# In the first chunk, ScalarE copies instead of DMAs fill two tiles' fixed value blocks, and the first two weight blocks are asked for earlier on GpSimd's queue

## The chip, the cores and the metric

The kernel runs on one core of one Trainium2 chip. The metric is the device time of one execution in microseconds (us); less is better. The core's engines run side by side, each in its own program order: TensorE (PE: matmuls, and PEld: the weight load ahead of each), VectorE (DVE), ScalarE (ACT), GpSimd (POOL) and SyncE (SP, which here only issues DMAs). They wait for each other on semaphores. Sixteen DMA engines move data between memory (HBM) and SBUF. POOL's DMAs go through the queue that the profile calls q0, SP's through q1; q8 carries instructions (75 packets of together 1.23 MB in this run).

## The reference

Block-sparse attention over 4 batches, 8 heads, 768 positions in 24 blocks of 32, then a two-layer network on its output:

```python
mask = |blk_i - blk_j| <= 1  or  blk_i in (0, 23)  or  blk_j in (0, 23)  or  blk_j in sampled_blocks[blk_i]
scores = where(mask, q @ k.T / sqrt(64), -1e9)
attn = softmax(scores)            # each row's sum + 1e-9 divides it
x = attn @ v                      # to [3072, 512]
out = relu(x @ w_in) ** 2 @ w_out # w_in 512 x 2048, w_out 2048 x 512
```

A query block so attends to the two fixed blocks 0 and 23, to three sampled blocks and to a window of three neighbours; the blocks 0 and 23 as queries attend to all keys. The weights come as float64 and are turned into float32 on the chip.

## The kernel before

A batch has 6 tiles of 128 queries; 3 tiles make a chunk, and there are 8 chunks. Everything is issued in an order written out by hand. The program first does the attention of chunk 0 alone (the tiles 0, 1 and 2 of batch 0, and the four head pairs of the "whole" queries), then for each chunk the network, with the next chunk's attention strewn between its matmuls. In the first part a half tile (`Half`, four heads) passes through scores (`s`, PE, L405), maxima (`m`, DVE, L417), exponentials (`p`, ACT, L464), transposes (`pt`, PE, L479), copies (`pT`, ACT, L489), the product with the values (`pv`, PE, L515) and the division (DVE). A whole query pair (`Whole`) passes through `g`, `mg`, `pg`, `ptg`, `pTg` and `pvg` in the same way; its `pTg` is copied half by ACT and half by DVE (L675). The loop over `work` at the end issues these stages in steps of `now`.

The values of tile k stand in two SBUF tiles, `V[k][0]` and `V[k][1]`. For each of 4 query blocks j there are, in rows of 32: in the first the two fixed blocks (rows 0 to 63) and two sampled ones, in the second a sampled one and the window. In the order listings V_83 and V_84 are the two of tile 0, V_127 and V_128 of tile 1, V_129 and V_130 of tile 2. Who fills them in chunk 0:

- SP's DMAs (q1), in this order: the query tiles q_0 and q_1, the fixed blocks of tile 0 for j = 0 (`load_static`, L214), its window (L313), the sampled blocks of tiles 0 and 1 (`load_sampled`, L327: 9 and 12 DMAs of 32 rows each), the fixed blocks of tiles 1 and 2 (`load_static`, two DMAs of 64 rows by 4 blocks j by 520 columns, which read the same 64 rows of `v` four times), q_2, and the sampled blocks of tile 2 (12 DMAs). Each of SP's DMAs reuses one of eight semaphores in turn and so waits until the DMA eight before it has landed.
- ACT: for tile 0 it copies the fixed blocks from j = 0 to j = 1, 2, 3 (`copy_static`, L221, two copies, one for each half of the heads). The list `fixed` is worked off at one entry per step from step 7 on. Later ACT places 12 window blocks of tile 1 (L229).
- POOL: the other window blocks (L229).

POOL also issues the loads of keys and values (`KN`, `vn`), copies sampled keys from `KN` to `KG` (`copy_keys`, L301 and L281), and asks for the weight blocks. `cut_next` (L786 for the DMA) handles one step of a row of weight blocks of 512 KB each: it loads one (`craw`, on POOL's queue) and turns the one loaded five steps earlier (ACT L802 and L804, then DVE L813 and L814, then the splits). The first five calls stand between POOL's copies of keys and windows and only load; the later ones stand in the `work` loop from step 35 on. At the change the program reads:

```python
    load_sampled(1, 0, nc.sync, SP)
    for k in range(1, UC):
        load_static(k, k // 2)
    load_q(0, 2, own=begin)
...
    for k in range(2):
        deque(copy_keys(0, k), 0)
    for i in range(AHEAD + 1):
        if i == FIRST_LOADS:
            for f, *at in windows[1, 0]:
                f(*at, nc.gpsimd.tensor_copy)
```

The network of chunk 0 begins with the transposes `xt` (L872), their copies `xh`, `xl` (L875, L876) and the first matmuls `ph` (L886); `po` (L915, L926) is its second layer.

Of the kernel before, what the change touches and what calls it, by code (L numbers as in the profile page):

```python
# [48 lines left out]
UC = 3  # L49
# [4 lines left out]
AHEAD = 5  # L54
# [29 lines left out]
LATE = (0, 4)  # L84
KEYS_N = 2
MOVED = 6


WO_LOW = 3
# [8 lines left out]
def tile_block_sparse_attention_moe(ctx: ExitStack, tc, kd, knd, qd, qgd, vd, vnd, samp, const, wcat, out):  # L98
# [86 lines left out]
    def values_of(k):  # L185

        return V[k if k < UC else 0]
# [4 lines left out]
    def halves(k, u):  # L192

        if k < UC:
            return slice(0, 2) if u == k // 2 else None
        return slice(u, u + 1)

    def columns(src, us):

        n = HW // 2  # L200
        return src[..., us.start * n : us.stop * n]

    def places(v, rows, js, us):

        return columns(v[rows, js].rearrange("p j u c -> p j (u c)"), us)

    def load_static(k, u, eng=nc.sync):
        us = halves(k, u)
        if us is None:
            return  # L210
        n = 1 if k == 0 else NJ
        src = columns(vd[order[k][0], V_STATIC * BLK :], us)
        src = src.unsqueeze(1).broadcast_to([2 * BLK, n, src.shape[-1]])
        eng.dma_start(places(values_of(k)[0], slice(0, 2 * BLK), slice(0, n), us), src)  # L214
# [40 lines left out]
    def load_q(b, t, eng=nc.sync, own=None):  # L255
        q = (own or rot).tile([P, NJ, NPAIR, BLK], F32, tag="q", name=f"q{b}_{t}", bufs=1 if own else 2)
        n = NJ * NPAIR * BLK
        eng.dma_start(q.rearrange("p a b c -> p (a b c)"), qd[b, :, t * n : (t + 1) * n])
        st["q", b, t] = q
# [9 lines left out]
    def copy_keys(b, t, own=None):  # L269

        vals = sampled(t, 0, POOL)
        kg = keys_of(b, t, own)
        for us in (slice(0, 1), slice(1, 2)) if t == 0 else (slice(0, 2),):
            if t < UC:
                for u in range(us.start, us.stop):
                    static_keys(b, t, u, nc.gpsimd.tensor_copy)
            for j in sorted(groups(t)):
                for r in range(NRAND):
                    to = kg[:, j, 2 + r].rearrange("p (u i) s -> p u (i s)", u=2)
                    of = KN.rearrange("p u k i s -> p u k (i s)")  # L280
                    nc.gpsimd.tensor_copy(to[:, us].unsqueeze(2), of[:, us, bass.ds(vals[NRAND * j + r], 1)])  # L281
                yield
# [32 lines left out]
    def load_sampled(k, u, eng, on):  # L315
        us = halves(k, u)
        if us is None:
            return
        b, t = order[k]
        VA, VB = values_of(k)  # L320
        vals = sampled(t, 1, on)
        v4 = columns(vd[b], us).rearrange("(a p) c -> p a c", p=BLK)
        for j in sorted(groups(t)):
            for r in range(NRAND):
                at = slice(0, BLK) if r == 2 else slice((2 + r) * BLK, (3 + r) * BLK)
                dst = places(VB if r == 2 else VA, at, slice(j, j + 1), us)
                eng.dma_start(dst, v4[:, bass.ds(vals[NRAND * j + r], 1)])  # L327
# [10 lines left out]
    def written(b, t):  # L338

        parts[b, t] = parts.get((b, t), 0) + 1  # L340
        whole = 2 + (NPAIR if t in (0, NT - 1) else 0)
        if parts[b, t] < whole or order.index((b, t)) < MOVED:
            return
# [9 lines left out]
    class Half:  # L353


        def __init__(self, b, t, u):
            self.b, self.t, self.u = b, t, u
            self.k = order.index((b, t))
            self.moved = self.k >= MOVED
            self.name = f"{b}_{t}_{u}"  # L360
# [469 lines left out]
    def cut_next():  # L830

        nonlocal done
        n = len(cuts)
        for stage, lag in ((cut, AHEAD), (cut_bits, AHEAD + 1), (cut_split, AHEAD + 2), (cut_load, 0)):
            if 0 <= done - lag < n:
                stage(*cuts[done - lag])
        done += 1
# [21 lines left out]
    def turn(c):  # L859
# [3 lines left out]
        for i in range(UC):  # L863
            if c * UC >= MOVED:
                while full:
# [129 lines left out]
    load_q(0, 1)  # L995
    load_sampled(0, 0, nc.sync, SP)
    load_sampled(1, 0, nc.sync, SP)
    for k in range(1, UC):
        load_static(k, k // 2)
    load_q(0, 2, own=begin)  # L1000
    load_sampled(2, 1, nc.sync, SP)
    windows = {
# [1 line left out]
        for k in range(1, UC)  # L1004
        for u in range(2)
    }
    for k in range(2):
        deque(copy_keys(0, k), 0)
    for i in range(AHEAD + 1):
# [3 lines that stand above are left out]
        if i == SECOND_LOADS:  # L1013
            deque(copy_keys(0, 2, begin), 0)
        if i == THIRD_LOADS:
            for f, *at in windows[2, 0] + windows[2, 1]:
                f(*at, nc.gpsimd.tensor_copy)
        if i < AHEAD:
            cut_next()
    fixed = [(copy_static, 0, i) for i in range(2)]  # L1020
    moves = windows[1, 1]
    side = lambda name: ps_o.tile([P, 512], F32, tag="o", name=name)
    work = Stream()
# [97 lines left out]
```

## Time and profile before

| | |
|---|---|
| timed runs | 746.91 us median of 3 (742.52, 746.91, 747.28) |
| the profiled execution | 743.47 us in all, of which the span of its instructions is 741.7 us |
| busy in the span | PE 713.3 us (96%), ACT 510.3, DVE 509.1, POOL 485.4 |
| attention of chunk 0 alone | from 0 to 58.25 us, when the first `ph` matmul starts |
| HBM traffic | 85.59 MB read, 6.29 MB written |
| granted TensorE clock | 0.995 of full speed over the span |

How to read the rows: a timeline row has the start and the length of a stretch of like instructions, in us from the start of the span, then engine, line, operation, what is written and read, the shape and the count; in brackets the idle time of the engine ahead of it, and what ended that. "issue" there means that the engine waited for nothing that the profile shows. A row of windows has a stretch, its length, each engine's busy time and, in brackets, how many of its instructions started in it, then the granted clock, the busy share of the DMA engines and the rate. A row of a DMA queue has packets, MB and the share of the 16 DMA engines' time in the stretch that was asked for. Most fp32 matmuls of the program are two in the records, transposes one.

### The profile page before, as it was taken

To read this page: it belongs to the slowest core of one execution; us is meant where nothing else is said; L and a number is where in the kernel's file an instruction comes from. 1 tells how busy PE (TensorE), PEld (TensorE's weight loads), DVE (VectorE), ACT (ScalarE), POOL (GpSimd) and SP (SyncE) were. 2 spreads that over 40 slices of the span, in tenths; PEclk is the share of its full clock that TensorE was granted. 3 is DMA by queue.
4 is the path that set the end of the run, shared out by engine and by line. 5 is a ranking of instruction groups with operands and counts; after the bars stand their busy time and mean duration, and the time that the engine had idled before them with its cause. 6 is when DMAs were issued, how large, how long until landed. Compare 5 with 4: busy or idle time off the path is not lost.

```text
span 741.7 us, 25152 instructions
## 1 busy us (share of the span) xinstructions
PE 713.3 (96%) x9440; PEld 591.5 (80%) x9440; DVE 509.1 (69%) x980; ACT 510.3 (69%) x1130; POOL 485.4 (65%) x592
## 2 busy tenths in 40 slices
PE   5779999999999999999999999999999999999997
PEld 2557676668888888887888888877888888889896
DVE  5776886767866866778876676778877677545342
ACT  3777887998867775689866777479876777623222
POOL 5984534237876565758767566677866566767784
PEclk9999999999999999999999999999999999999999
DMA  8986889643533535533444345534344342101001
GB/s 279 235 224 186 262 256 331 150 116 107 141 82 96 144 90 168 155 86 113 105 125 106 98 118 166 158 86 141 93 126 105 89 131 53 33 2 43 1 1 43
DMA packets 84861, 93.54 MB, mean 126 GB/s; under 512 B 13539, under 2 KB 70628, under 8 KB 84740
## 3 DMA queue, kind: packets, MB, share of 16 engines
q1 hardware_dynamic: 78788, 69.09, 35.3%
q0 software_dynamic: 5664, 22.45, 9.3%
q8 instruction: 75, 1.23, 0.7%
q14 instruction: 46, 0.38, 0.2%
q10 hardware_dynamic: 288, 0.39, 0.1%
HBM read 85.59 MB, written 6.29 MB: 124 GB/s over the span
## 4 chain that ended last, share of the span: by engine, by line
PE 84%; DVE 4%; ACT 4%; issue 1%; ACTq 0%; DVEq 0%
PE ph L886 35%; PE po L926 31%; PE s L405 6%; PE pv L500 5%; PE po L915 4%; PE pvg L689 1%; PE g L621 1%; DVE xl L876 1%; ACT craw L804 1%; DVE WO L814 1%; DVE m L417 0%; PE pv L515 0%; DVE WO L813 0%; PE pt L479 0%; ACT p L464 0%
## 5 line engine op out<-in xcount | busy, mean ns | idle before, releaser
L450 ACT ACTIVATE pm<-p 32x256 f32<-32x256 f32 x528 | 219.2, 415 | 17.3 <-DVE p L425 9.6
L849 POOL TENSOR_TENSOR wo<-WO,wo 128x512 fp32r<-128x512 f32 x112 | 144.8, 1293 | 61.3 <-DVE wo L848 60.0
L849 POOL TENSOR_TENSOR wi<-W,wi 128x512 fp32r<-128x512 f32 x104 | 135.1, 1299 | 66.8 <-ACT wi L846 32.8
L886 PE MATMUL ph<-xh,wi 128*128 128x384 f32 x832 | 175.6, 348 | 2.0 <-DVE wi L848 1.7
L926 PE MATMUL po<-wo,gh 128*128 128x512 f32 x672 | 176.2, 397 | 0.0
L890 ACT ACTIVATE r<-ph 128x384 f32<-128x384 f32 x128 | 62.7, 490 | 162.8 <-PE ph L886 162.1
L905 POOL TENSOR_TENSOR gl<-gf,gh 128x384 fp32r<-128x384 f32 x112 | 113.8, 1016 | 85.1 <-DVE gf L902 73.1
L886 PEld LDWEIGHTS ph<-xh,wi 128*128 128x128 f32 x832 | 146.9, 188 | 22.8 <-issue 10.1
L902 DVE SCALAR_TENSOR_TENSOR gf<-ph,r 128x384 f32<-128x384 f32 x112 | 62.3, 556 | 147.3 <-ACT r L890 142.6
L926 PEld LDWEIGHTS po<-wo,gh 128*128 128x128 f32 x672 | 123.8, 188 | 24.4 <-issue 4.0
L926 PE MATMUL po<-wo,gl 128*128 128x512 f32 x336 | 98.3, 401 | 0.0
L886 PE MATMUL ph<-xl,wi 128*128 128x384 f32 x416 | 90.4, 339 | 0.0
L926 PEld LDWEIGHTS po<-wo,gl 128*128 128x128 f32 x336 | 62.2, 189 | 17.0 <-issue 2.8
L886 PEld LDWEIGHTS ph<-xl,wi 128*128 128x128 f32 x416 | 73.9, 188 | 2.0 <-issue 1.9
L848 DVE TENSOR_REDUCE wo<-WO 128x512 fp32r<-128x512 f32 x112 | 74.7, 667 | 0.0
L417 DVE TENSOR_REDUCE m<-s 128x2 f32<-128x512 f32 (+1 forms) x96 | 61.6, 683 | 13.7 <-PE s L405 13.7
L897 ACT ACTIVATE gh<-r 128x384 fp32r<-128x384 f32 x112 | 58.9, 526 | 10.2 <-POOL wo L849 0.7
L848 DVE TENSOR_REDUCE wi<-W 128x512 fp32r<-128x512 f32 x91 | 60.9, 669 | 0.0
L405 PE MATMUL s<-KG,q 64*32 64x160 f32 x1408 | 49.2, 309 | 0.9 <-ACT KG L301 0.9
L425 DVE TENSOR_TENSOR p<-s,m 128x512 f32<-128x512 f32 (+1 forms) x72 | 45.9, 679 | 0.0
L915 PE MATMUL po<-WO,gp 128*128 128x512 f32 x96 | 44.8, 601 | 0.0
L456 DVE STREAM_TRANSPOSE pT<-pm 128x1024 f32<-128x1024 f32 (+1 forms) x36 | 41.2, 1144 | 0.0
(96 smaller groups left out, 873.2 us busy)
## 6 DMA issues: line engine op xcount, KB each, us to landing
craw<-in_w_dram POOLq DMA_DIRECT2D x32, 512.0 KB, 5.8
V<-in_v_dram SPq DMA_DIRECT2D x462, 32.5 KB, 1.9
KG<-in_k_dram SPq DMA_DIRECT2D x198, 64.0 KB, 2.0
V<-in_v_dram SPq DMA_DIRECT2D x28, 390.0 KB, 4.3
q<-in_q_dram SPq DMA_DIRECT2D x24, 256.0 KB, 2.8
out_dram<-ot SPq DMA_DIRECT2D x22, 256.0 KB, 2.6
V<-in_v_dram SPq DMA_DIRECT2D x14, 292.5 KB, 4.1
vn<-in_vn_dram SPq DMA_DIRECT2D x5, 780.0 KB, 5.6
```

Of the source, the lines that this page charges most:

```text
L405: nc.tensor.matmul(self.sb[e][g * BLK : (g + 1) * BLK, i * NSLOT + a : i * NSLOT + z], q[r, j, pr, :], k, start=True, stop=True,)
L417: nc.vector.tensor_reduce(m[at, e], self.sb[e][at].rearrange("p (i c) -> p i c", i=2), axis=AX, op=ALU.max)
L450: nc.scalar.activation(p[a * BLK : (a + 1) * BLK, g], x[g * BLK : (g + 1) * BLK, :, a], AF.Exp, scale=SCALE)
L848: nc.vector.tensor_reduce(w[:, 0], src.unsqueeze(2), axis=AX, op=ALU.max)
L849: nc.gpsimd.tensor_tensor(w[:, 1], src, w[:, 0], op=ALU.subtract)
L886: nc.tensor.matmul(ph[:, :TOK], w, x, start=(i == 0), stop=(i == len(steps) - 1))
L890: nc.scalar.activation(r, ph[:, :TOK], AF.Relu)
L897: nc.scalar.activation(gh, r, AF.Square)
L902: nc.vector.scalar_tensor_tensor(gf, ph[:, :TOK], 0.0, r, op0=ALU.max, op1=ALU.mult)
L905: nc.gpsimd.tensor_tensor(gl, gf, gh, op=ALU.subtract)
L915: nc.tensor.matmul(acc[c][u], g[:, u * P : (u + 1) * P], WO[f], start=(f == 0), stop=(f == NF - 1))
L926: nc.tensor.matmul(acc[c][u], g[:, at], w[:, k], start=first, stop=(f == NF - 1 and g is gl))
```

## The change

```diff
@@ constants
+EARLY_CUTS = 2
@@ the main body, first loads
     load_q(0, 1)
     load_sampled(0, 0, nc.sync, SP)
     load_sampled(1, 0, nc.sync, SP)
-    for k in range(1, UC):
-        load_static(k, k // 2)
     load_q(0, 2, own=begin)
     load_sampled(2, 1, nc.sync, SP)
@@
+    for _ in range(EARLY_CUTS):
+        cut_next()
     for k in range(2):
         deque(copy_keys(0, k), 0)
     for i in range(AHEAD + 1):
@@
-        if i < AHEAD:
+        if EARLY_CUTS <= i < AHEAD:
             cut_next()
-    fixed = [(copy_static, 0, i) for i in range(2)]
+    fixed = [(copy_static, k, i) for k in range(UC) for i in range(2)]
```

Two DMAs leave SP's queue. Four copies of 64 rows by 4 x 260 columns come to ACT, with tile 0's loaded block as their source. The first two loads of weights move on POOL ahead of the key copies; the number of loads and the blocks are the same. PE's and DVE's instructions and their order don't change. Lines of the changed program are one further down.

ACT in the first steps (`pg` exponentials and `pTg` copies of the whole queries, `p` exponentials of tile 0), before:

```order
L645 ACTIVATE pg_0_443<-g_0_1_427,mg_0_436 128x384
L221 COPY V_83<-V_83 64x3x260 x2
L675 COPY pTg_0_473<-ptg_0_0_457 128x384
L645 ACTIVATE pg_1_476<-g_1_0_446,mg_1_465 128x384
L645 ACTIVATE pg_1_476<-g_1_1_447,mg_1_465 128x384
L675 COPY pTg_1_552<-ptg_1_0_530 128x384
L464 ACTIVATE p_0_0_541<-s_0_0_0_479,m_0_0_538 96x256 x2
```

The same place now:

```order
L646 ACTIVATE pg_0_441<-g_0_1_425,mg_0_434 128x384
L222 COPY V_83<-V_83 64x3x260 x2
L222 COPY V_127<-V_83 64x4x260
L676 COPY pTg_0_472<-ptg_0_0_455 128x384
L646 ACTIVATE pg_1_475<-g_1_0_444,mg_1_463 128x384
L646 ACTIVATE pg_1_475<-g_1_1_445,mg_1_463 128x384
L222 COPY V_127<-V_83 64x4x260
L222 COPY V_129<-V_83 64x4x260 x2
L676 COPY pTg_1_554<-ptg_1_0_532 128x384
L465 ACTIVATE p_0_0_543<-s_0_0_0_479,m_0_0_540 96x256 x2
```

One new copy stands ahead of the first `pTg`, and three stand ahead of the second `pTg` and of the first exponentials of tile 0.

SP's queue at the end of tile 1's sampled blocks, before (ISA rows set registers):

```order
L327 DMA V_128<-in_v_dram 32x520
L214 DMA V_127<-in_v_dram 64x4x520
L214 DMA V_129<-in_v_dram 64x4x520
L258 DMA q_2_217<-in_q_dram 128x512
L247 TENSOR_LOAD idx
L327 ISA
L327 DMA V_129<-in_v_dram 32x520
```

Now:

```order
L328 DMA V_128<-in_v_dram 32x520
L259 DMA q_2_215<-in_q_dram 128x512
L248 TENSOR_LOAD idx
L328 ISA
L328 DMA V_129<-in_v_dram 32x520
```

q_2 follows the sampled blocks of tile 1 at once, and everything behind it on SP moves up by two DMAs.

POOL after its first loads, before:

```order
L182 DMA KN<-in_kn_dram 128x1536
L234 DMA vn_1_139<-in_vn_dram 128x1560
L247 TENSOR_LOAD idx
L301 COPY KG_98<-KN 128x4x2x64
L281 ISA
```

Now:

```order
L183 DMA KN<-in_kn_dram 128x1536
L235 DMA vn_1_139<-in_vn_dram 128x1560
L787 DMA craw_0_254<-in_w_dram 128x1024
L787 DMA craw_0_256<-in_w_dram 128x1024
L248 TENSOR_LOAD idx
L302 COPY KG_98<-KN 128x4x2x64
```

The two weight loads now follow the value load on the same queue, ahead of the wait for the first keys.

## Prediction

> **What bounds the kernel now.** I read the page's chain of waits first, then windows over the span, then PE's timeline in the first 58 us, and the DMA queues where PE stood still.
>
> ```profile
> PE 84%; DVE 4%; ACT 4%; issue 1%; ACTq 0%; DVEq 0%
> 20.00:40.00 20.00, 12.46 (x404) 0.91 0.91 234
> 58.25:741.70 683.45, 675.15 (x8396) 1.00 0.42 116
> ```
>
> The chain is PE's. From 58.25 us on PE is busy for 675.15 of 683.45 us, and the change touches nothing there. So it is worth what it moves the first `ph` matmul, at 58.25 us. Ahead of that PE has holes: it is busy for 12.46 us of the stretch from 20 to 40. The timeline shows the large ones:
>
> ```profile
> 27.13 0.94 PE L689 MATMUL pvg<-vn,pTg 128*32 128x65 f32 x33 [2.06 <-issue]
> 32.45 0.54 PE L689 MATMUL pvg<-vn,pTg 128*32 128x65 f32 x23 [0.76 <-issue]
> 34.88 0.87 PE L515 MATMUL pv<-V,pT 128*32 128x65 f32 x32
> 39.57 0.54 PE L515 MATMUL pv<-V,pT 128*32 128x65 f32 x16 [3.82 <-issue]
> 48.86 0.77 PE L515 MATMUL pv<-V,pT 128*32 128x65 f32 x36 [1.37 <-issue]
> 58.25 0.96 PE L886 MATMUL ph<-xh,WI 128*128 128x384 f32 x4 [0.82 <-ACT xh L875]
> ```
>
> Four holes, 8.0 us in sum, are put down to nothing that the profile shows. Each lies inside a `pvg` or `pv` that had begun (the third after 32 of 48 matmuls), so operands were not what was missing. Windows cut at the holes show what these share, and the queues show what ended the third:
>
> ```profile
> 27.12:32.44 5.32, 4.56 (x128) 3.55 (x127) 3.15 (x9) 3.35 (x9) 5.09 (x19) 0.68 0.91 232
> 32.44:39.56 7.12, 3.29 (x127) 2.67 (x128) 3.39 (x11) 3.81 (x9) 6.37 (x17) 1.00 0.91 230
> 39.56:43.90 4.34, 4.33 (x124) 3.48 (x127) 3.35 (x8) 3.12 (x8) 4.16 (x12) 0.67 0.56 137
> ...
> q1 hardware_dynamic: 388, 0.71, 74.4%
> q0 software_dynamic: 118, 0.46, 30.9%
> ...
> q8 instruction: 1, 0.02, 5.8%
> ...
> q1 hardware_dynamic: 59, 0.09, 32.9%
> ...
> q8 instruction: 1, 0.02, 5.9%
> ```
>
> Hole to hole PE starts 127 or 128 matmuls and as many weight loads, some 256 instructions: a block. The queue rows are of four stretches: 32.45 to 36.95 us (DMA engines full, no packet of q8), 36.95 to 38.3 (one packet of q8; PE goes on at 39.57), 39.57 to 40.85 (a third busy, none of q8), 40.85 to 42.5 (one). I read them so: PE's next block of instructions is asked for when PE enters a block. Behind full DMA engines its packet starts 4.5 us later, with idle ones 1.3; PE goes on at most 2.6 us after that. The block from 39.56 had no hole and took 4.3 us, the one ahead of it 7.1. The Trainium skill (Runtime: NRT & Kernel Launch, "Instruction fetch mechanics") has 16 KiB blocks of 256 instructions, as counted here, and calls a crossing mostly hidden; if that held here, the third hole would not be a fetch, which is the first rival below.
>
> **Part 1: two DMAs fewer on SP.**
>
> ```profile
> 27.33 1.36 SPq L214 DMA_DIRECT2D V<-in_v_dram  x2
> 28.74 0.67 SPq L258 DMA_DIRECT2D q<-in_q_dram  x1
> 30.86 12.41 SPq L327 DMA_DIRECT2D V<-in_v_dram  x12
> 43.38 0.92 SPq L258 DMA_DIRECT2D q<-in_q_dram  x2
> ...
> q1 hardware_dynamic: 551, 1.08, 98.5%
> ```
>
> The two take SP 1.4 us. The queue row is of 29 to 34.3 us: 551 packets of q1 alone fill the DMA engines for 5.3 us. The two DMAs have 2 x 64 rows x 4 = 512 packets, most of these. This traffic stands ahead of the fetch that ends the third hole. Without it the block from 32.45 needs the larger of its work, 3.3 us, and a fetch behind light traffic, 4.3; the second pair of weight blocks and tile 2's sampled rows are still about, so I take 4.6 instead of 7.1: **2.5 us less** (bounds: nothing, if the remaining traffic delays the fetch as much, and 3.8, the hole itself). SP reaches q_2 1.4 us earlier and can issue tile 2's 12 sampled blocks, which took 12.41 us amid the traffic, faster; q_3, q_4 (43.38) and tile 3's window, whose buffers are free by then, come up to 8 us sooner. They meet the next fetch, which had idle engines: the block from 39.56 takes 5.0 us, as the next one does (43.90 to 48.86), instead of 4.3: **0.7 us more** (bounds 0 to 1.4). q_2 and tile 2's values are wanted only after the third hole, so nothing is late for them.
>
> **Part 2: four copies more on ACT.**
>
> ```profile
> 10.61 1.57 ACT L221 COPY V<-V 64x780 f32<-64x780 f32 x2
> 12.09 0.47 ACT L675 COPY pTg<-ptg 128x384 f32<-128x384 f32 x1
> 12.46 1.05 ACT L645 ACTIVATE pg<-g,mg 128x384 f32<-128x384 f32 x2
> 15.11 0.48 ACT L675 COPY pTg<-ptg 128x384 f32<-128x384 f32 x1 [1.61 <-PE ptg L669]
> 15.86 1.55 ACT L464 ACTIVATE p<-s,m 96x256 f32<-96x256 f32 x4 [0.27 <-DVE m L422]
> 21.21 1.24 ACT L229 COPY V<-vn 32x260 f32<-32x260 f32 x3
> ...
> 17.93 0.88 PE L689 MATMUL pvg<-vn,pTg 128*32 128x65 f32 x46 [1.48 <-DVE pTg L675]
> 18.74 0.88 PE L479 MATMUL pt<-ident,p 96*128 96x96 f32 x8
> 20.57 1.11 PE L515 MATMUL pv<-V,pT 128*32 128x65 f32 x48
> ```
>
> A copy of 780 columns takes about 0.84 us here and one of 260 about 0.41, so 520 columns cost 0.43, and 1040 columns some 1.06 us: 4.2 us for four. The first moves the first `pTg` from 12.09 to 13.15 and the `pg` pair behind it to 13.5 to 14.6, about when PE wants them. The other three end at 17.7, so the second `pTg` starts 2.6 us late (17.7), and the exponentials of tile 0 end at 19.75 instead of 17.41. PE stood for 1.48 us until 17.93 for DVE's half of this `pTg`, and its transposes `pt` came only at 18.74. So `pvg` moves to 18.25 and the last `pt` ends at 20.0 instead of 19.6: **0.4 us late** at `pv`, and 2.6 us if that wait of PE's did not cover it (the upper bound; below, nothing). After that ACT waits for PE again and has the time back.
>
> **Part 3: two weight loads 15 us earlier.**
>
> ```profile
> 35.75 0.69 ACT L802 ACTIVATE ct<-craw 128x512 f32<-128x512 f32 x1
> 6.31 0.61 POOL L301 COPY KG<-KN 128x512 f32<-128x512 f32 x1 [2.31 <-DMA KN<-in_kn_dram]
> 19.14 1.04 POOL L786 DMA_DIRECT2D craw<-in_w_dram  x2
> ...
> q0 software_dynamic: 221, 1.25, 72.9%
> q1 hardware_dynamic: 214, 0.45, 30.3%
> ...
> q1 hardware_dynamic: 429, 0.66, 103.7%
> ...
> q1 hardware_dynamic: 170, 0.22, 34.4%
> ...
> q0 software_dynamic: 280, 1.05, 81.3%
> ```
>
> The two issues fit into POOL's wait of 2.31 us for the first keys, and POOL is 1 us earlier from 19 us on: free, since its next products have slack. The first block is used only at 35.75, so nothing gains from their landing. What changes is whom the 1.05 MB meet. The queue rows are of 9 to 14 us, 15 to 17.2, 17.3 to 20 and 20 to 24.2. The blocks leave the last of these, where the fetch ahead of the first hole waited. They follow `vn` on q0, so start at about 15 us, where q1 has the DMA engines to itself and brings q_1 and tile 0's sampled blocks, which `pv` needs at 20.57 and no earlier. From 9 to 14 us both queues moved as many packets (221 and 214). Taking turns so, 256 packets of the blocks and 256 of q1, 1.58 MB at some 340 GB/s, last from 15 to 19.6; the remaining 150 or so of q1's go through by 20.7, and land by 21.6. So `pv` starts at **21.7 instead of 20.57**, with ACT's 0.4 us inside this (bounds: 21.0, ACT's alone, and 23, if a late fetch comes in front of it as well). The skill's DMA: Bandwidth & Descriptors ("Queues, rings and completion order") has each DMA engine take turns between queues packet by packet, which the row of 9 to 14 us bears out; it speaks against this part.
>
> **The sum**, at PE's block boundaries:
>
> - From `pv` at 20.57 to the first hole PE took 4.5 us (25.07). From 21.7 it comes there at 26.2; the fetch no longer meets weights and is there by then (asked for at about 21.2, plus 4.3). 27.13 becomes 26.2: 0.9 us won.
> - The next block takes 4.8 instead of 5.3, since the third weight block comes 1 us earlier: 0.5 won.
> - Part 1: 2.5 won, 0.7 lost.
>
> 0.9 + 0.5 + 2.5 - 0.7 = 3.2 us. The rest keeps its length, since ACT paces it:
>
> ```profile
> 43.90:58.25 14.35, 10.88 (x332) 9.04 (x322) 11.52 (x25) 12.64 (x26) 9.16 (x25) 0.98 0.97 283
> ```
>
> ACT is busy there for 12.64 of 14.35 us. So `ph` starts at 55.05, the span becomes 738.5 us, and the profiled execution, 743.47 (1.8 around its span), becomes 740.3. The four executions shown lie at 742.52, 743.47, 746.91 and 747.28, their middle at 745.2, 1.7 above the profiled one; for a median I predict 745.2 - 3.2 = **742.0 us**.
>
> **Rivals.**
>
> - *The holes don't come from traffic.* If a fetch takes its time whatever the queues do, or the third hole is something else, only part 2's 0.4 us and perhaps the first hole's 0.9 stay: within 0.5 us of before, 745. For it: the hole of 1.37 us at 48.86 stands in a stretch that the change leaves alone, and the second came 2.4 us behind a request amid traffic. Against: 4.5 against 1.3 us to the packet. 20%.
> - *The early start loses more than the later part wins (slower).* Part 3's collision at 15 to 20 us, with the fetch due at about 20 us behind the same packets: `pv` at 23, 2.4 late, and the first hole's end at 27.6 to 28. It decides if the third hole then shrinks by less than 1 us, because q_3, q_4 and tile 3's window, now unhindered, fill the engines instead. The price: 2.4 - 0.9, some 1.5 us, 746.7. 15%.
> - *All holes go.* With `pv` only 0.4 late and blocks of 4.3 us the sum grows by 0.7 at the start, 0.5 and 0.3 in the two blocks ahead of 39.57, 0.7 in the next and half a us at 48.86: 5.9 won, 739.3. Against: ACT's 12.64 us above. 10%.
> - That the change does nothing at all is excluded by the order of its instructions.
>
> **How the numbers follow.** The forecast, 1 to 5 us won, holds 55%. A measurement of this kernel tells about 1%, 7.5 us, from no change; no case reaches it by itself. With the spread of 4.8 us between equal runs, the third rival and the upper end of the forecast may: faster 7%, slower 4%, within 1% 89%. The range goes from 745.2 - 6 and another 1.7 for a profiled-like run to the highest run shown with nothing won: 737.5 to 747.5. The forecast's own range is 740 to 744.
>
> **What would show it.** In the changed profile: ACT copies of 64x1040 at about 1.06 us and the second `pTg` at about 17.7; `craw` packets on q0 from about 15 us, and `pv` of tile 0 at 21 to 23; no hole of 2 us near 25; the hole of 3.82 us down to about 1; `ph` first at 53 to 57. The prediction is wrong if that hole stays above 2.5 us with q1 light ahead of it, if `pv` comes after 23, or if `ph` comes 2 us earlier and the end doesn't.

## The result and the profile after

| | before | the change |
|---|---|---|
| median of 13 executions | 746.91 us (742.52 to 748.47) | 742.08 us (739.63 to 746.44) |
| ratio of the change to before | | 0.9948, 95% interval 0.9926 to 0.9970 |
| profiled execution | 743.47 us, span 741.7 | 742.89 us, span 741.1 |
| first `ph` matmul | 58.25 us | 55.80 us |
| from there to the span's end | 683.45 us | 685.30 us |

By medians 4.8 us are won, by the ratio 3.9 (2.2 to 5.5). The two profiled executions differ by 0.6 us alone: the one of before is near the fast end of its executions, the one of the change above its median. The start shows what changed; the last row, which should not have changed, is taken up under "Why the prediction held".

The page of the change, chain of waits first, then windows over the span (length, then busy time and count of PE, PEld, DVE, ACT, POOL, the granted clock, the DMA engines' share, GB/s):

```profile
PE 84%; DVE 4%; ACT 4%; issue 1%; ACTq 0%; DVEq 0%
```

```profile
20.00:40.00 20.00, 16.66 (x543) 12.66 (x535) 16.36 (x46) 16.94 (x39) 18.51 (x49) 0.91 0.58 167
55.80:741.00 685.20, 675.66 (x8396) 563.50 (x8396) 470.59 (x871) 473.30 (x1052) 441.57 (x461) 1.00 0.41 116
```

The chain is what it was. From 20 to 40 us PE now gets through 543 matmuls in 16.66 us, where it had 404 in 12.46, and the DMA engines are busy for 0.58 of the stretch instead of 0.91. PE's timeline (start, length, form, count, the idle time ahead and what ended it):

```profile
17.84 1.04 PE L690 MATMUL pvg<-vn,pTg 128*32 128x65 f32 x48 [1.46 <-ACT pTg L676]
18.81 0.88 PE L480 MATMUL pt<-ident,p 96*128 96x96 f32 x8
22.50 0.27 PE L516 MATMUL pv<-V,pT 128*32 128x65 f32 x2 [1.56 <-DMA V<-in_v_dram]
23.03 1.20 PE L516 MATMUL pv<-V,pT 128*32 128x65 f32 x46 [0.25 <-DMA V<-in_v_dram]
...
27.43 0.99 PE L690 MATMUL pvg<-vn,pTg 128*32 128x65 f32 x48
...
35.09 0.53 PE L516 MATMUL pv<-V,pT 128*32 128x65 f32 x15 [0.24 <-issue]
...
39.15 0.64 PE L516 MATMUL pv<-V,pT 128*32 128x65 f32 x26 [0.66 <-issue]
...
45.10 1.30 PE L516 MATMUL pv<-V,pT 128*32 128x65 f32 x36 [2.57 <-issue]
46.33 1.97 PE L480 MATMUL pt<-ident,p 128*128 128x128 f32 x8
...
55.80 0.98 PE L887 MATMUL ph<-xh,WI 128*128 128x384 f32 x4 [0.82 <-ACT xh L876]
...
59.01 0.49 PE L406 MATMUL s<-KG,q 64*32 64x160 f32 x10 [1.17 <-issue]
```

Nothing puts an idle time to "issue" near 25 us any more (2.06 before) or near 32 (0.76). The third hole went from 3.82 to 0.24 us, at 35.09 instead of 39.57. The block behind it starts at 39.15 instead of 43.90. There PE is 4.5 to 4.75 us ahead. Then it loses 2.3 of them: the last hole grew from 1.37 to 2.57 us, and the eight `pt` behind it took 1.97 us, where a full-rate group takes 1.09. Windows cut at PE's block ends show the same stretches, and in the last one the matmuls behind the last hole:

```profile
22.50:27.75 5.25, 4.99 (x118) 3.83 (x122) 2.37 (x8) 2.63 (x7) 5.04 (x15) 0.67 0.60 174
27.75:31.55 3.80, 3.17 (x142) 2.49 (x135) 3.62 (x11) 3.46 (x10) 3.57 (x12) 1.00 0.79 225
31.55:35.09 3.54, 3.31 (x143) 2.68 (x132) 3.36 (x11) 3.49 (x10) 3.16 (x9) 1.00 0.59 193
35.09:39.15 4.06, 3.40 (x126) 2.73 (x126) 3.85 (x9) 4.06 (x9) 3.73 (x8) 1.00 0.43 117
39.15:45.10 5.95, 3.38 (x126) 2.71 (x127) 4.58 (x11) 5.17 (x11) 5.72 (x19) 0.97 0.84 252
45.10:48.23 3.13, 3.13 (x44) 2.62 (x43) 1.72 (x4) 0.58 (x1) 3.13 (x12) 0.51 0.80 226
```

PE's own work in a block is 3.2 to 3.4 us in the four from 27.75, at a granted clock of 0.97 to 1.00; in the one from 22.50, at 0.67, it is 4.99. The block that took 7.12 us now takes 3.54, and the one that meets a DMA share of 0.84 takes 5.95. The DMA queues of the change (packets, MB, share), four stretches: 32.5 to 33.0 us, 36 to 37, 39.15 to 42.6 and 42.6 to 43.7:

```profile
q1 hardware_dynamic: 60, 0.09, 52.8%
q8 instruction: 1, 0.02, 13.7%
...
q8 instruction: 1, 0.02, 5.8%
...
q1 hardware_dynamic: 651, 0.88, 82.9%
...
q8 instruction: 1, 0.02, 5.3%
```

In two blocks the instruction packet came 1 to 2 us after PE had entered (31.55 to 32.5-33.0; 35.09 to 36-37). In the second the traffic was light (a share of 0.43). In the first the DMA engines were 91% busy until the packet came, and light after it (0.59 over the block), so little can have been left in the queues. In the full stretch from 39.15 none came for 3.4 us, and PE went on at 45.10, at most 2.5 us after it. What filled that stretch stands on SP, whose rows are its DMA issues:

```profile
38.29 0.84 SPq L259 DMA_DIRECT2D q<-in_q_dram  x2
39.18 0.42 SPq L314 DMA_DIRECT2D V<-in_v_dram  x1
```

q_3, q_4 and the 390 KB window of tile 3 were issued at 38.3 to 39.2, five us sooner than before (43.38), so they now meet this fetch. At the start, ACT and POOL:

```profile
10.69 2.54 ACT L222 COPY V<-V 64x780 f32<-64x780 f32 x3
14.43 2.98 ACT L222 COPY V<-V 64x1040 f32<-64x1040 f32 x3
17.30 0.49 ACT L676 COPY pTg<-ptg 128x384 f32<-128x384 f32 x1
17.67 1.57 ACT L465 ACTIVATE p<-s,m 96x256 f32<-96x256 f32 x4
```

```profile
4.00 1.04 POOL L787 DMA_DIRECT2D craw<-in_w_dram  x2
6.39 0.61 POOL L302 COPY KG<-KN 128x512 f32<-128x512 f32 x1 [1.35 <-DMA KN<-in_kn_dram]
```

Three copies take 2.98 us, the second `pTg` starts at 17.30 and the exponentials end at 19.24. POOL still waits 1.35 us for the keys, so the two issues cost it nothing.

### The profile page after: what moved, and what is told of

Its sections match the earlier page's. It is cut to its first block, busy times and chain, and to the rows that moved or that the text cites. A ratio compares the mean times of both kernels' runs of the same rounds, so it can differ in the third digit from the quotient of the medians.

```text
span 741.1 us, 25155 instructions
## 1 busy us (share of the span) xinstructions
PE 714.4 (96%) x9440; PEld 591.9 (80%) x9440; DVE 511.0 (69%) x980; ACT 513.9 (69%) x1134; POOL 485.2 (65%) x592
## 4 chain that ended last, share of the span: by engine, by line
PE 84%; DVE 4%; ACT 4%; issue 1%; ACTq 0%; DVEq 0%
PE ph L887 35%; PE po L927 31%; PE s L406 6%; PE pv L501 5%; PE po L916 4%; PE pvg L690 1%; PE g L622 1%; ACT craw L805 1%; DVE xl L877 1%; DVE WO L815 1%; DVE m L418 0%; PE pv L516 0%; DVE WO L814 0%; PE pt L480 0%; ACT p L465 0%
## 6 DMA issues: line engine op xcount, KB each, us to landing
V<-in_v_dram SPq DMA_DIRECT2D x462, 32.5 KB, 1.8
```

## The experiments

**The theory** is the prediction's: the large holes are fetches of PE's next block of instructions, about 127 matmuls with their weight loads, which wait behind other DMA traffic; the two DMAs removed were that traffic ahead of the third hole. **The rivals:** a fetch takes its time whatever the queues do; the holes are waits for operands; or the two early weight loads, not the copies, brought the gain. All ratios are to the kernel before, on the same chip; `ph` is the start of the first `ph` matmul in the kernel's profile. A median of 9 to 13 executions is uncertain by some 2 us; each kernel has one profile.

**1. copies_only: the ACT copies without the early weights.**

```diff
-EARLY_CUTS = 2
+EARLY_CUTS = 0
```

> The change with its second part undone: ScalarE still places the fixed blocks and the two DMAs are gone, but the first two weight blocks are asked for where they were, at 19 us. If PE's holes are waits for its next block of instructions behind DMA traffic, the hole of about 2 us near 25 us comes back (the fetch meets the weights at 20 to 24 us), tile 0's first pv starts at 21.0 instead of 22.5 (no collision with the weights at 15 to 20 us), and the hole that was 3.82 us stays below 1. First ph at 55 to 57 us, the median between 741 and 744. If the gain came from the earlier weights instead, first ph is at 58 and the median at 746 to 747, as before.

Measured 745.08 us, ratio 0.9957 (0.9929 to 0.9985), `ph` at 55.95. PE's timeline:

```profile
27.70 0.66 PE L690 MATMUL pvg<-vn,pTg 128*32 128x65 f32 x32 [2.74 <-issue]
...
37.12 0.53 PE L516 MATMUL pv<-V,pT 128*32 128x65 f32 x15 [0.81 <-issue]
```

The third hole is down from 3.82 to 0.81 us and the first one stands (2.74): the copies shorten the third, the early weights the first. `ph` is where the change has it. The median was expected lower; the interval of the ratio overlaps the change's.

**2. early_only: the early weights without the copies.** The two DMAs are back behind tile 1's sampled blocks, and ACT copies only what it copied before.

```diff
     load_sampled(1, 0, nc.sync, SP)
+    for k in range(1, UC):
+        load_static(k, k // 2)
-    fixed = [(copy_static, k, i) for k in range(UC) for i in range(2)]
+    fixed = [(copy_static, 0, i) for i in range(2)]
```

> The change with its first part undone: the two DMAs place the fixed blocks again, and only the two weight loads are early. By the theory of traffic the hole near 25 us is gone, pv of tile 0 starts at 22 to 22.5, and the hole at 36 to 40 us is back with 3 to 4 us, since 29 to 34 us is full of the two DMAs: first ph at 57.5 to 59, the median at 745 to 748. If the third hole belonged to the weights' place in the queue or to ScalarE's order, it stays below 1.5 us and the median is about 742.

Measured 747.59 us, ratio 1.0008 (0.9982 to 1.0034), `ph` at 58.20: nothing won.

```profile
22.82 0.27 PE L516 MATMUL pv<-V,pT 128*32 128x65 f32 x2 [3.04 <-DMA V<-in_v_dram]
...
39.85 0.54 PE L516 MATMUL pv<-V,pT 128*32 128x65 f32 x16 [4.55 <-issue]
```

`pv` of tile 0 is 2.25 us late with nothing else changed ahead of it, so that delay is the early weights'. The hole near 25 us went, and the third one took it back: 4.55 us. With run 1 this says that the copies carry the gain and the early weights none: the ratios are 0.9957 with the copies alone and 1.0008 with the weights alone.

**3. traffic_back: the change, with as much other traffic at that place.** Four loads of 128 rows by 512 columns go onto SP's queue where the two DMAs stood. Nobody reads what they bring; the rest is the change.

```diff
     load_sampled(1, 0, nc.sync, SP)
+    for f in (11, 13, 14, 15):
+        nc.sync.dma_start(W1[f], vd[0, (NVB - NJ) * BLK :, :DM])
```

> The change with four loads added on SP where the two DMAs stood: 1.05 MB in 512 packets of 2 KB into buffers of weights that are not yet in use; nobody reads or waits for them before the weights are written there much later. If traffic delays the fetch, the hole of some 3 us comes back at the same matmul, first ph is at 57.5 to 59.5 and the median 745 to 748. If the gain came from PE, SP or POOL no longer waiting for those two DMAs, nothing waits here either: the hole stays below 1 us, first ph at about 56, the median at 742.

```profile
39.07 0.86 PE L516 MATMUL pv<-V,pT 128*32 128x65 f32 x15 [3.82 <-issue]
```

The hole is back at 3.82 us, at the same matmul, with no instruction of PE, ACT, DVE or POOL changed: traffic makes it. `ph` comes at 59.05. The time missed the expectation (745 to 748): 744.24 us, ratio 0.9967 (0.9936 to 0.9997), as if the hole cost nothing. The profiled execution took 751.15. It is among the slowest of a wide lot (741.78 to 752.57), and its later part had three holes more, shown below. Whether the faster executions had the third hole is not known.

**4. shift_blocks: before, with the block ends moved.** 32 transposes of the identity are put first on PE; nobody reads them. With their weight loads they are a quarter of a block.

```diff
+    first = bank("first")
+    for i in range(32):
+        nc.tensor.transpose(first[:, :P], ident, ident)
```

> The kernel before, with 32 transposes of the identity added as PE's first work, in its idle time ahead of 6 us. If the holes are ends of PE's instruction blocks, each moves 32 matmuls and 32 weight loads up in PE's program: the hole that split the second tile 0 pv after 32 of 48 matmuls now stands at the end of the scores ahead of it, and the one that split pvg after 15 of 48 stands in the scores ahead of that. If they are waits for something that those products read, they stay at the same matmuls. The time stays within 3 us of before either way.

Measured 745.01 us, ratio 0.9981 (0.9955 to 1.0007, which takes in no change), `ph` at 56.72.

```profile
32.41 1.10 PE L515 MATMUL pv<-V,pT 128*32 128x65 f32 x47 [0.81 <-issue]
...
38.00 0.40 PE L405 MATMUL s<-KN,q 64*32 64x96 f32 x16 [3.45 <-DMA q<-in_q_dram]
...
40.05 1.89 PE L515 MATMUL pv<-V,pT 128*32 128x65 f32 x58 [0.60 <-issue]
```

The hole stood after 32 matmuls of its `pv`; it now stands after one. The others moved by 31 or 32 as well. An operand does not become late at another matmul because PE did 32 others at the start; the end of a block does. The hole also shrank. Counted back 128 matmuls, its fetch was asked for at about 27.7 us, when SP was only issuing the two DMAs (from 27.56). But the traffic then held q_2, which follows them on SP, and PE waited 3.45 us for that.

**5. change_again: the change, unedited**, for the spread.

> The change once more, unedited, for a second profile and for times on the chip of the other three. By the theory the holes stand where they stood, in the matmuls after 25 us: none of 2 us near 25, below 1 us at 35 and 39, about 2.5 us near 45; first ph between 55 and 57 us, the median 741 to 744. If the first ph moves by more than 2 us between two profiles of the same program, the single profiles here can't carry what is read from them.

Measured 744.53 us, ratio 0.9971 (0.9947 to 0.9996), `ph` at 58.29. The third hole was 0.25 us, as in the first profile. The last one was 1.20 us and not the expected 2.5, and one stretch behind it differed. DVE and PE:

```profile
46.09 2.98 DVE L814 SCALAR_TENSOR_TENSOR W<-W,craw 128x512 int32<-128x512 int32 x1
49.11 2.69 DVE L815 SCALAR_TENSOR_TENSOR W<-craw,W 128x512 int32<-128x512 int32 x1
```

```profile
44.53 0.77 PE L516 MATMUL pv<-V,pT 128*32 128x65 f32 x36 [1.20 <-issue]
...
52.68 2.18 PE L516 MATMUL pv<-V,pT 128*32 128x65 f32 x64 [3.35 <-DVE x L547]
```

Two DVE operations that take 0.69 us each in quiet stretches took 2.98 and 2.69, and PE's next `pv` waited 3.35 us for DVE. One profile's `ph` is therefore worth about 2.5 us either way, and the size of its last hole about 1.4.

**6. one_early: one early weight load instead of two.**

```diff
-EARLY_CUTS = 2
+EARLY_CUTS = 1
```

> The change with one early weight block instead of two; the second is asked for at 19 us, as before. Half as much traffic meets tile 0's sampled blocks: its first pv starts at 21 to 21.9 instead of 22.5. The fetch near 25 us meets one block instead of two: no hole there, or below 1 us. By the theory of traffic first ph comes 0.5 to 1.2 us earlier than in the change, at 54.6 to 55.4, and the median 0.5 to 1 us below the change's. If only the amount of traffic in the first 25 us counts and not its place, ph stays at 55.8.

Measured 743.12 us, ratio 0.9961 (0.9937 to 0.9984), `ph` at 55.30. Eight matmuls of `pv` started at 21.03, but the rest waited until 23.78 for values: half the early traffic did not halve the delay. Not told apart from the change.

**7. shift_change: the change with the 32 transposes of run 4.**

> The change with 32 transposes of the identity as PE's first work, in its idle time, so that every block of instructions ends 32 matmuls earlier in PE's program. By the theory the holes move up by 32 matmuls, and their sizes change with what the DMA engines carry when the next block is asked for: the one of 2.57 us at 45 us moves into the scores or values ahead of it. First ph between 54 and 57 us, the median within 2 us of the change's, to either side. If the holes belong to the products, they stay at their matmuls.

Measured 740.85 us, ratio 0.9932 (0.9908 to 0.9955), `ph` at 52.34.

```profile
30.01 0.47 PE L406 MATMUL s<-KG,q 64*32 64x160 f32 x7 [0.34 <-issue]
...
41.35 0.46 PE L406 MATMUL s<-KG,q 64*32 64x160 f32 x3 [0.47 <-issue]
```

These are its only fetch holes after tile 0. The transposes hold the first `g` back from 6.38 to 8.85 us, and `ph` still comes 3.5 us sooner. That is more than expected: `ph` is ahead of 54, and the median 3.7 us under change_again's, where 2 were the most.

**8. fifth_early: the change, with a fifth weight block sent for a third step earlier.** Two blocks are then issued at 29.36 on POOL, instead of one at 29.05.

```diff
-FIRST_LOADS, SECOND_LOADS, THIRD_LOADS = 2, 3, 4
+FIRST_LOADS, SECOND_LOADS, THIRD_LOADS = 2, 3, 5
```

> The change with the fifth weight block asked for right behind the fourth, at about 29.6 us instead of 41, ahead of POOL's window copies of tile 2. By the theory of traffic the fetch that was asked for at 31.5 us now stands behind two blocks: the hole at 35 us grows from 0.24 to some 1 to 2 us; the one at 45 us shrinks from 2.57 to 1.5 to 2.2, since q_3, q_4 and tile 3's window alone stand ahead of that fetch. First ph within 1 us of the change's 55.8, the median within 1.5 us of the change's. If weights weren't what delays fetches, both holes stay.

Measured 744.77 us, ratio 0.9969 (0.9946 to 0.9992), `ph` at 56.24.

```profile
38.22 0.53 PE L516 MATMUL pv<-V,pT 128*32 128x65 f32 x15 [2.91 <-issue]
```

512 KB moved ahead of the third fetch made 2.91 us of 0.24, more than the 1 to 2 expected. Traffic of another queue and engine does the same as SP's. The last hole was 1.47 us, but change_again has 1.20 there with nothing taken away, so this says nothing about it.

**9. shift_whole_block: the change with 128 transposes**, of 32 by 32. With their weight loads they are one whole block, so the later ends fall where the change has them.

```diff
+    for i in range(128):
+        nc.tensor.transpose(first[:BLK, :BLK], ident[:BLK, :BLK], ident[:BLK, :BLK])
```

> The change with 128 small transposes (32 by 32) of the identity as PE's first work: 256 instructions, one whole block, so that the blocks end at the same matmuls as in the change, while PE does as much early work as with 32 large ones. If the gain of the shift by 32 came from where blocks end, it is gone: holes at the change's matmuls (below 1 us at the first two in tile 1's pv, 1 to 2.6 us in the fourth), first ph at 55 to 58.5 us, the median 742 to 745. If it came from PE's early work (its clock, or the first block fetched sooner), first ph is at 52 to 54 and the median near 741.

Measured 744.93 us, ratio 0.9967 (0.9943 to 0.9992), `ph` at 56.15.

```profile
32.33 0.54 PE L690 MATMUL pvg<-vn,pTg 128*32 128x65 f32 x23 [0.41 <-issue]
37.53 0.53 PE L516 MATMUL pv<-V,pT 128*32 128x65 f32 x15 [1.90 <-issue]
41.58 0.65 PE L516 MATMUL pv<-V,pT 128*32 128x65 f32 x26 [0.66 <-issue]
45.61 0.76 PE L516 MATMUL pv<-V,pT 128*32 128x65 f32 x36 [0.64 <-issue]
```

The holes are back at the change's own matmuls (15, 26 and 36 left of a `pv`), 3.6 us in sum against the 0.8 of run 7. Two were not of the expected size: 1.90 where less than 1 was expected, and 0.64 where it was 1 to 2.6. The granted clock was 1.00 from 20 us to `ph` in both kernels. So run 7 gains by where the blocks end, not by PE being at work early. The 128 transposes also start `pv` of tile 0 later, at 24.09 (run 7: two matmuls at 23.10, the rest at 23.79), which is 0.3 to 1 us of the 3.8 between the two `ph`.

**10 and 11. shift_one_early and shift_copies_only**: the 32 transposes with one early weight load, and with none (`EARLY_CUTS` 1 and 0).

> The change with one early weight block instead of two and with the shift by 32 transposes. With the shift, the first pv of tile 0 waited for its sampled values until 23.8 us; with half of the early traffic it starts at 21.5 to 22.5. If the rest stays as in the shifted change, first ph is at 51 to 52.3 us and the median 739 to 741. If the second block, asked for at 19 us, delays the fetch that is asked for at about 21, a hole of 1 us or more stands there and ph is at 52.5 to 54.

> The change without its early weights (both blocks asked for at 19 us) and with the shift by 32. By the theory of traffic the fetch asked for near 20 us meets the two blocks at 20 to 24 us; its block now ends 32 matmuls earlier, so the hole of 2.74 us seen without the shift comes earlier by these and is of 1.5 to 3 us. First ph at 53 to 55 us, the median 741 to 743.5. If the early weights matter nothing once the blocks are shifted, ph is at 52.3 or earlier, since tile 0's pv then starts at 21.

Measured 741.59 us, ratio 0.9917 (0.9887 to 0.9946), `ph` at 51.85; and 738.45 us, ratio 0.9882 (0.9837 to 0.9927; 6 executions), `ph` at 51.96. In the profile of shift_copies_only the hole near 25 us that run 1 has at 2.74 became two:

```profile
25.59 0.27 PE L406 MATMUL s<-KN,q 64*32 64x96 f32 x2 [0.45 <-issue]
30.39 0.47 PE L406 MATMUL s<-KG,q 64*32 64x160 f32 x7 [1.35 <-issue]
```

These are some 1.5 us more than run 7 has (0.34 at 30.01), and yet `ph` is no later than there: `pv` of tile 0 starts at 22.50 and does not wait again until 23.79. The early weights win nothing with the blocks moved either. `ph` and the median of shift_copies_only are below what was expected first (53 to 55; 741 to 743.5); the median of shift_one_early is just above its 739 to 741. shift_copies_only is the fastest measured: its median is 738.45 us against 747.69 of the kernel before on that chip and 742.08 and 744.53 of the change, and its ratio's interval meets the change's (0.9926 to 0.9970) only at the last digit. From shift_one_early it is not told apart.

## Why the prediction held

The forecast was 3.2 us less, and 742.0. Measured are 3.9 (2.2 to 5.5) and 742.08. That the medians agree to 0.1 us is luck: the forecast started from 745.2, where the 13 executions of before have 746.91, so the gain was as much too small as the start was too low, and change_again has 744.53.

The cause of the third hole is the one named. In one profile each, traffic_back and fifth_early bring it back by traffic alone, and shift_blocks moves it with the blocks. That the time won comes from this hole is not shown: traffic_back, which has the hole and `ph` at 59.05, has a ratio of 0.9967, and the change 0.9948 and 0.9971. For it speak early_only, with the hole and 1.0008, and the three shifted kernels of the change, which have the earliest `ph` and the lowest ratios. The sum came out through terms that were wrong both ways.

- **Part 1, third hole: right and under-sized.** 2.5 us were forecast for the block from 32.45; it went from 7.12 to 3.54, so 3.6. The step that failed is "a fetch behind light traffic, 4.3", raised to 4.6 for traffic that was still about. The 4.3 was no time of a fetch: in the prediction's own row of 39.56 to 43.90 PE is busy for 4.33 of the 4.34 us, at a granted clock of 0.67, so it was the length of PE's work. The packet came 1 to 1.5 us after the block was entered and PE went on about 2.1 to 2.6 us later, so 3.5 in all.
- **Part 1, next block: no loss.** 0.7 us were to be lost at the block from 39.56 (4.34); it takes 4.06. A hole of 0.66 us is new, but PE's work in it takes 3.40 us at a granted clock of 1.00, instead of 4.33 at 0.67. The forecast had left out the clock. q_3, q_4 and tile 3's window came sooner, as forecast, but met the fetch one block later than forecast: that block took 5.95 us instead of 4.96, and PE then ran at a granted clock of 0.51 for 3.1 us. In change_again, where they were issued from 39.72 to 41.04, this block took 4.58 us (39.95 to 44.53), so that they always cost as much is not shown.
- **"The rest keeps its length, since ACT paces it": wrong.** From 43.90 to 58.25 PE took 14.35 us; the same work now took 16.65, from 39.15 to 55.80. The 12.64 us that ACT was busy there are no floor that a fetch hole adds nothing to: the hole and the slow matmuls came on top, and so may have a DVE operation that took 2.70 us at 48.50 instead of 0.69. shift_change, without that hole, has `ph` at 52.34.
- **Part 2: right, and cheaper.** 17.7 was forecast for the second `pTg` and 19.75 for the end of the exponentials; 17.30 and 19.24 are measured. `pvg` came at 17.84 against 17.93, the `pt` at 18.81 against 18.74. At `pv` copies_only, which has no early weights, shows what the copies cost alone: 20.86 against 20.57, 0.3 us instead of 0.4.
- **Part 3: right in kind, half the size.** `pv` of tile 0 was forecast at 21.7, within 21.0 and 23. It began at 22.50 and waited again until 23.03, so 1.9 us late, and 2.4 for all but two matmuls, instead of 1.1; early_only gives 2.25 for the start by the weights alone. The queues of the change, 15 to 19 us and 19 to 23:

```profile
q0 software_dynamic: 275, 1.01, 70.7%
q1 hardware_dynamic: 271, 0.43, 31.5%
...
q1 hardware_dynamic: 371, 0.52, 49.7%
```

The turn-taking from 15 to 19.6 came as forecast. The step that failed is what was left for q1 behind it, "the remaining 150 or so", through by 20.7 and landed by 21.6: q1 moved 371 packets from 19 to 23 us, and `pv` waited for values until 23.03. How many of them were tile 0's the rows don't say. The hole near 25 went, as forecast, but PE came to that block's end at about 27.75 (the 16th of the 48 matmuls from 27.43) instead of 26.2, 0.6 us lost where 0.9 were to be won. The block behind it took 3.8 us instead of 5.3: 1.5 won instead of 0.5. Here too the clock had a part: before, 0.68 was granted in the block from 27.12 to 32.44; now that block has 1.00, and the one ahead of it, from 22.50 to 27.75, has 0.67.

At the third hole's end the sum is thus 4.5 us won (39.57 to 35.09), against 3.9 forecast; at `ph` it is 2.45, against 3.2.

The slower rival had the early start right (`pv` at 23), but not its condition: the third hole shrank by 3.6 us, not by less than 1. The rival in which all holes go forecast 5.9 us, `ph` at 52.35: the change doesn't reach it, but the three shifted kernels made from it do, at 51.85 to 52.34.

**The last row of the result's table.** From `ph` to the span's end the 13 profiles have 683.25 to 690.35 us, though that part of the program is equal. Some of it is more fetch holes, which come in one execution and not in another: the unedited change has one of 1.17 us at 59.01 in its first profile, and one of 1.14 at 241.35 in its second. PE's timeline of traffic_back, the longest of them:

```profile
62.68 0.49 PE L406 MATMUL s<-KG,q 64*32 64x160 f32 x10 [1.61 <-issue]
...
244.06 0.46 PE L406 MATMUL s<-KG,q 64*32 64x160 f32 x3 [1.14 <-issue]
...
559.47 0.50 PE L406 MATMUL s<-KG,q 64*32 64x160 f32 x14 [1.67 <-issue]
```

These 4.4 us stand in the scores `s`. The profile of before has none of them, which fits its place near its fast end. The four shifted kernels whose ends moved by 32 have none in `s` either. The hole of 1.17 is part of why a gain of 2.45 us at `ph` showed as 0.6 at the end of that profile. Whether such holes also make the 4 us by medians is not shown. What else makes executions differ by several us, and why the median of traffic_back is lower than its `ph` suggests, stays open.

## What to carry to other kernels

When idle time is put down to nothing but issue and recurs every 127 or 128 short matmuls, suspect the fetch of instructions. Here it was that, and what shortened it was less DMA traffic when a block began, or another place for the block's end. Traffic that is removed there lets later transfers come sooner, so look at which fetch they meet next. Look at the granted clock of a stretch before its length is taken for a wait: 4.3 us of matmuls at 0.67 were read as a fetch here. Judge a change of this size by medians: two profiles of the same program differ by 2.5 us at `ph`, and the 13 profiles by up to 7 behind it.

## What the runs showed of the hardware

- An instruction packet of 16 KB came 1 to 2 us after PE had entered the change's blocks from 31.55 and 35.09, and at least 3.4 us and 4.5 us after it had entered two whose stretch stayed full (39.15 in the change, 32.45 before). PE went on at most 2.6 us after it there, and some 3 us after it in shift_blocks (29.2 to 32.41). Busy DMA engines alone don't tell the delay: in the change's block from 27.75, with a share of 0.91 until then, the packet came within 1 us. The Trainium skill (Runtime: NRT & Kernel Launch, "Instruction fetch mechanics") calls a crossing mostly hidden. Where a block is 3.4 us of short matmuls, as here, that holds for holes like that of 0.24 us in the change, and not with the traffic that before, early_only, traffic_back and fifth_early have ahead of the third fetch (2.91 to 4.55).
- 32 useless transposes that move the block ends lowered the ratio further when added to the change: 0.9932, 0.9917 and 0.9882 with them, 0.9948 (0.9971 in change_again), 0.9961 and 0.9957 without, for two, one and no early weight loads. Added to the kernel before they gave 0.9981, which is not told from no change.
- An int32 DVE operation of 128x512 that takes 0.69 us took 2.70 in the change and up to 2.98 in change_again, beside POOL's work and DMA issues. What holds it was not tried.
- After the hole of 2.57 us the next eight `pt` took 1.97 us instead of 1.09, at a granted clock of 0.51 from 45.10 to 48.23. The blocks behind the holes of 2.06 and 3.82 us before had 0.68 and 0.67. Not every hole is followed by this: behind the 2.91 us of fifth_early the clock was 1.00 (38.22 to 42.00).
